# Attention scores by pairs of key blocks: full passes against high queries, half passes against low queries

## The chip, the cores and the metric

The kernel runs on one core of one Trainium2 chip. The metric is the device time of one execution in microseconds (us); lower is better.

## What is computed

The kernel is a chain of three layers. The change lies in the first, an attention without softmax over 8 batches of 3072 rows:

```python
def _attn_ref(u, v, z) -> np.ndarray:
    B, S, D = u.shape            # 8, 3072, 256
    d_qk = z.shape[-1]           # 64
    scale = 1.0 / S
    scores = scale * np.matmul(z, z.transpose(0, 2, 1))
    attn = np.maximum(scores, 0.0) ** 2
    out = np.matmul(attn, v)
    return (u * out).astype(np.float32)
...
    x = attn_out.reshape(B * S, D)
    x = _moe_ref(x=x, **moe_kwargs)
    return _moe2_ref(x=x, **moe2_kwargs)
```

Queries and keys are the same z, so the scores are symmetric. `_moe_ref` is a dense layer (256 to 1024, softmax-like gate, layer norm, back to 256), `_moe2_ref` routes each row to one of 8 experts.

## The kernel before

**Precision.** All data is float32. A float32r matmul rounds its inputs, so each operand is split into a high part (the rounded value) and a low part (the rest). A product of two split operands is three matmuls, high with high, high with low, low with high (`mm3`, L107 to L110).

**Tiling.** Queries go by chunks of 512 (`CH`), six a batch, 48 in all (`NCHUNK`). Keys go by blocks of 128 rows (`P`), 24 for each chunk (`NKB`), so the attention has 48 x 24 = 1152 slots. One slot handles one key block of one chunk. For the block of slot n the scores are computed four slots ahead (`LA`), ScalarE takes the Relu out of PSUM (`act_relu`, L432), squares it and rounds it to ah (L437, L442), VectorE makes the low part al (L447), and TensorE adds six matmuls to the chunk's output o (`pe_av`, through L108 to L110).

**Symmetry.** A block whose mirror image has been computed for an earlier chunk of the batch is not computed again: it was kept in DRAM, is fetched three slots ahead (`get`, L410) and transposed by VectorE where needed. Of a batch's 144 slots 88 are computed, 704 in all. The buffers through which kept blocks go out and come back are a ring (`sym_b`, L349 to L352) of `NSYM` = 8; each write and each fetch takes the next place of the ring (`sym`, L383).

**The scores.** z has only 64 columns. `load_z` puts the transposed chunk of z twice on the 128 partitions, and `prep_z` (L282) turns the upper 64 into the high part and the lower 64 into the low part: the tile zw is [high; low]. `swap_z` (L296) lets GpSimd write the same chunk upside down for the queries: zv is [low; high]. A score block is then two matmuls over all 128 rows (`pe_scores`, L421): zw's block against zw gives high x high + low x low, and against zv high x low + low x high. Each score block is a PSUM buffer of its own; `ps_s` has two of them (L142), so that the scores of a computed block wait for the Relu of the computed block before the last.

**Order.** Nothing is scheduled by a tool. The loop at the end (L1047) walks the slots and issues for each, in this order, the scores of slot n + 4 (if that block is computed), the steps that were entered for this slot (the dense layer of the chunk before, the loads, `prep_z`, `swap_z` five slots before a chunk's first scores), `pe_av` of slot n, then Relu, square and split. Each engine works through its instructions in that order. The routed experts come after the attention, from about 3070 us on; they reuse the buffers of zw and zv (`take`, L764).

Of the kernel before, what the change touches and what calls it, by code (L numbers as in the profile page):

```python
# [10 lines left out]
F32 = mybir.dt.float32  # L11
F32R = mybir.dt.float32r
# [4 lines left out]
AF = mybir.ActivationFunctionType  # L17
ALU = mybir.AluOpType
# [3 lines left out]
P = 128  # L22
CH = 512
# [10 lines left out]
def attention_moe_kernel(ctx, tc, u, v, z, w_in, w_out, g_ln, w_gate, w1, w2, out):  # L34
    nc = tc.nc
    B, S, D = u.shape
    DZ = z.shape[2]
# [6 lines left out]
    NCB = S // CH  # L44
    NKB = S // P
# [3 lines left out]
    NA = 4  # L49
    ZB = 5  # L50
    GA = 3
    NSYM = 8
    PD = 1
    ZL = 8
    XA, XT0, XE = 2, 21, 23
# [45 lines left out]
    V, A, G, T = nc.vector, nc.scalar, nc.gpsimd, nc.tensor  # L101
# [30 lines left out]
    with ExitStack() as st:  # L132
        wts = st.enter_context(tc.tile_pool(name="wts", bufs=1))
        zp = st.enter_context(tc.tile_pool(name="zp", bufs=NCB))
# [7 lines left out]
        ps_s = st.enter_context(tc.tile_pool(name="ps_s", bufs=2, space=PSUM))  # L142
# [21 lines left out]
        t = vp.tile([P, 2, 4, D], F32R, tag="vw", name="raw64").bitcast(I32).rearrange("p a r d -> p (a r d)")  # L164
        raw64 = [t[:, i * 2 * CH:(i + 1) * 2 * CH].rearrange("p (f two) -> p f two", two=2) for i in range(2)]
        t = mp.tile([P, F], F32, tag="pT", name="cu64").bitcast(I32)
        c64, u64 = t[:, :CH], t[:, CH:]
        t = [mp.tile([P, CH], F32R, tag=k, name="t64").bitcast(F32) for k in ("pth0", "ptl0", "pth1", "ptl1")]
# [92 lines left out]


        z_raw, v_raw, u_raw = {}, {}, {}
        z_t, z2_t, v_t = {}, {}, {}

        def rows(x, c):
            b, j = divmod(c, NCB)
# [12 lines left out]
            z_raw[c] = w  # L280

        def prep_z(c):  # L282
            zt = z_raw.pop(c)
            up_, low = slice(0, DZ), slice(DZ, 2 * DZ)
            w = zp.tile([P, CH], F32R, tag="zw", name="zw")
            A.activation(out=w, in_=zt, func=AF.Copy)
            if c == 0:
                w2_ = zp.tile([P, CH], F32R, tag="zv", name="zv", bufs=2)
                A.activation(out=w2_, in_=zt, func=AF.Copy)
                z2_t[c] = w2_  # L290
            V.tensor_tensor(out=w[low], in0=zt[low], in1=w[low].bitcast(F32), op=ALU.subtract)
            if c == 0:
                V.tensor_tensor(out=w2_[up_], in0=zt[up_], in1=w2_[up_].bitcast(F32), op=ALU.subtract)
            z_t[c] = w

        def swap_z(c):  # L296

            w = zp.tile([P, CH], F32R, tag="zv", name="zv", bufs=2)
            G.tensor_scalar(out=w[:DZ], in0=z_t[c][DZ:], scalar1=1.0, scalar2=1.0, op0=ALU.mult, op1=ALU.mult)
            G.tensor_scalar(out=w[DZ:], in0=z_t[c][:DZ], scalar1=1.0, scalar2=1.0, op0=ALU.mult, op1=ALU.mult)  # L300
            z2_t[c] = w

        def load_v(c, h):
            t = raw.tile([P, 2, D], F32, tag="vr", name="vr", bufs=2)
# [31 lines left out]
        def again(q, k):  # L336
            return q == NCB - 2 and k == NCB - 1
# [11 lines left out]
        t = [xrow.tile([P, KD * CH], F32, tag="x", name="sym") for _ in range(2)]  # L349
        t = [x[:, i * CH:(i + 1) * CH] for x in t for i in range(2)]  # L350
        t += [mp.tile([P, CH], F32, tag=f"sym{i}", name=f"sym{i}") for i in range(NSYM - 4)]
        sym_b = t  # L352
# [13 lines left out]
        def block(n):  # L366

            c, i = divmod(n, NKB)
            kb = orders[c][i]
            return (c // NCB) % 2, c % NCB, kb // 4, kb % 4  # L370

        def is_kept(n):
            _, q, k, _ = block(n)
            return k < q and not again(k, q)
# [44 lines left out]
        s_t, r_t, a_t, ah_t, al_t, o_t = {}, {}, {}, {}, {}, {}  # L419

        def pe_scores(n):  # L421
            c = n // NKB
            _, _, k, r = block(n)
            w = z_t[(c // NCB) * NCB + k][:, r * P:(r + 1) * P]
            s = ps_s.tile([P, CH], F32, tag="s", name="s")
            T.matmul(out=s, lhsT=w, rhs=z_t[c], start=True, stop=False)
            T.matmul(out=s, lhsT=w, rhs=z2_t[c], start=False, stop=True)  # L427
            s_t[n] = s

        def act_relu(n):  # L430
            r = ap.tile([P, CH], F32, tag="r", name="r")
# [323 lines left out]
        def own(pool, tag, shape, dt=F32R, bufs=None):  # L755
            return pool.tile(shape, dt, tag=tag, name=tag + "_x", **({"bufs": bufs} if bufs else {}))

        def own_vp():
            return own(vp, "vw", [P, 2, 4, D]).rearrange("p a r d -> p (a r d)")

        def cut4(t):
            return [t[:, i * CH:(i + 1) * CH] for i in range(4)]

        def take(name):  # L764

            if name in ("raw1", "raw2"):
                raw_w[name] = own_vp().bitcast(F32)
            elif name in ("w1h", "w1l", "w2h", "w2l"):
                w_set[0, name] = cut4(own_vp())
            elif name == "xT0":  # L770
                xT_t[0] = own_vp().rearrange("p (a k c) -> p a k c", a=2, k=KD)
            elif name == "xT1":
                xT_t[1] = own(mp, "xt", [P, 2, KD, CH])
            elif name == "hT":
                t = [own(zp, "zw", [P, CH]) for _ in range(NCB)]
                t += [own(zp, "zv", [P, CH], bufs=2) for _ in range(2)]
                hT_b.extend((t[i], t[i + 1]) for i in range(0, len(t) - 1, 2))
                o_b.extend(own(ap, "a", [P, CH], F32, bufs=NA).rearrange("p (r d) -> p r d", d=D) for _ in range(2))
            elif name == "out":
                t = own(mp, "p", [P, F], F32)  # L780
                o_b.extend(t[:, i * CH:(i + 1) * CH].rearrange("p (r d) -> p r d", d=D) for i in range(2))
            elif name == "set1":
                c = [own(raw, "zd", [P, CH], F32)]
                t = own(raw, "ur", [P, KD, CH], F32)
                c += [t[:, 0], t[:, 1]]
                c += [own(ap, "r", [P, CH], F32) for _ in range(2)] + [own(ap, "a", [P, CH], F32, bufs=NA), own(mp, "sym0", [P, CH], F32)]
                c += [own(mp, f"sym{i}", [P, CH], F32) for i in (1, 2)]
                c = [t.bitcast(F32R) for t in c]
                c += [own(ap, "ah", [P, CH], bufs=4) for _ in range(4)]
                c += [own(ap, "al", [P, CH], bufs=3) for _ in range(3)]  # L790
                for i, k in enumerate(("w1h", "w1l", "w2h", "w2l")):
                    w_set[1, k] = c[4 * i:4 * i + 4]
# [50 lines left out]
        for i in range(NU):  # L843
            w = HALF if i < N_CUT else units[i]
# [71 lines left out]
        for c in range(NCHUNK):  # L916
# [8 lines left out]
            else:  # L925
# [5 lines left out]
                at(base - 2, turn_z, c)  # L931
            at(zload, load_z, c)
            at(base, prep_z, c)
            if c > 0:
                at(s0 - LA - 5, swap_z, c)
# [12 lines left out]
            for t in range(4):  # L948
                w = s1 + 2 + (TW if last else 6) * t
# [8 lines left out]
                out_, back, cut_, y = (4, 6, 10, 12) if last else (5, 8, 12, 15) if c < NCHUNK - 3 else (5, 7, 10, 12)  # L958
                at(w + out_, blk_put, c, t)
                at(w + back, blk_get, c, t)  # L960
                cut_, y = w + cut_, w + y
# [32 lines left out]

        s0 = NS - NKB
        at(s0, take, "raw1")
        at(s0, load_w, 0, 1)
        at(s0 + 6, take, "w1h")
        at(s0 + 11, take, "w1l")
        at(s0 + 16, take, "raw2")  # L1000
        at(s0 + 16, load_w, 0, 2)
# [44 lines left out]
        with tc.manual_schedule():  # L1046
            for n in range(min(lo_slot, -LA), hi_slot + 1):  # L1047
                i = n + LA
                k = n - NS
                if 0 <= i < NS and not is_kept(i):  # L1050
                    pe_scores(i)
# [59 lines left out]
```

## Time and profile before

| | |
|---|---|
| median of 3 runs (lowest, highest) | 4315.48 us (4313.22, 4316.8) |
| profiled execution: own time, span of its core | 4313.29 us, 4311.6 us |
| TensorE, matmuls: busy, share, count | 4231.3 us, 98%, 23458 |
| TensorE, weight loads: busy, share | 3664.3 us, 85% |
| VectorE / ScalarE / GpSimd: share of the span | 74% / 65% / 28% |
| chain that ended last: TensorE, DMA, SP's queue, VectorE | 75%, 7%, 7%, 6% |

Rows of the profile name the line of the kernel, the engine (PE is TensorE, PEld its weight loads, DVE VectorE, ACT ScalarE, POOL GpSimd, SP the queue of the sync engine, which issues most DMAs), the operation, and output<-inputs by the program's names with their shapes. In a timeline the first number is the start and the second the length, in us. The end of a matmul is modelled: the next one can start before it. In a group, "xN | a, b | c" is N instructions, a us of busy time, b ns of one on average, and c us in which the engine stood idle just before them, with what ended that after "<-".

### The profile page before, as it was taken

The numbers are of one execution on the slowest core, as the hardware profiler recorded it, in microseconds if no ns is written. First come the engines' busy times: TensorE is split into PE (matmuls) and PEld (weight loads), VectorE is DVE, ScalarE is ACT, GpSimd is POOL, SyncE is SP. The second block draws the span as 40 slices with busy tenths as digits, with TensorE's granted clock in tenths as the row PEclk, the third lists the DMA queues.
The fourth block names the chain that finished last, engine by engine and source line by source line (L and its number), as shares of the span: only waits on it lengthen the run. The fifth ranks groups of instructions, "written<-read, shape, count | busy, mean of one in ns | idle before, by whom it ended". The sixth has DMA issues, their size and how long they took to land.

```text
span 4311.6 us, 74509 instructions
## 1 busy us (share of the span) xinstructions
PE 4231.3 (98%) x23458; PEld 3664.3 (85%) x23458; DVE 3197.2 (74%) x5624; ACT 2800.7 (65%) x5184; POOL 1200.7 (28%) x2486
## 2 busy tenths in 40 slices
PE   7999999999999999999999999999899999999999
PEld 5888888888888888888888888888788999999998
DVE  8777787777778787877877787777666656655686
ACT  6766776776677677667767766775444444444565
POOL 5023223322322332232233233323222111111111
PEclk9999999999999999999999999999999999999999
DMA  5799789889978988897898899789755655555575
GB/s 150 169 171 167 184 174 163 178 177 175 159 192 173 163 180 180 172 161 192 172 164 183 173 174 162 186 166 165 145 147 150 156 145 134 145 137 146 155 212 170
DMA packets 2465549, 719.23 MB, mean 167 GB/s; under 512 B 2261117, under 2 KB 2351485, under 8 KB 2465152
## 3 DMA queue, kind: packets, MB, share of 16 engines
q1 hardware_dynamic: 2441952, 654.93, 72.9%
q0 software_dynamic: 23200, 59.55, 4.4%
q8 instruction: 183, 3.00, 0.3%
q14 instruction: 214, 1.75, 0.1%
HBM read 442.46 MB, written 273.49 MB: 166 GB/s over the span
## 4 chain that ended last, share of the span: by engine, by line
PE 75%; DMA 7%; SPq 7%; DVE 6%; issue 2%; ACT 2%; POOL 0%; DVEq 0%; POOLq 0%; ACTq 0%
PE o L109 10%; PE o L108 10%; PE o L110 9%; SPq L410 4%; PE y L109 3%; PE y L108 3%; PE y L110 3%; PE g L108 3%; PE yp L108 3%; PE g L109 3%; PE yp L110 3%; PE yp L109 3%; PE h L494 3%; PE h L495 3%; PE h L498 3%; PE g L110 3%
## 5 line engine op out<-in xcount | busy, mean ns | idle before, releaser
L109 PE MATMUL o<-al,vw 128*128 128x512 f32 x2304 | 912.8, 396 | 26.6 <-DVE al L447 26.0
L108 PE MATMUL o<-ah,vw 128*128 128x512 f32 x2304 | 910.4, 395 | 3.0 <-DVE ut L471 2.8
L110 PE MATMUL o<-ah,vw 128*128 128x512 f32 x2304 | 900.7, 391 | 0.0
L442 ACT ACTIVATE ah<-a 128x512 fp32r<-128x512 f32 x832 | 526.0, 632 | 201.1 <-DVE a L416 77.1
L432 ACT ACTIVATE r<-s 128x512 f32<-128x512 f32 x704 | 415.3, 590 | 344.8 <-PE s L427 327.1
L447 DVE TENSOR_TENSOR al<-a,ah 128x512 fp32r<-128x512 f32 x832 | 575.5, 692 | 1.0
L109 PEld LDWEIGHTS o<-al,vw 128*128 128x128 f32 x2304 | 434.6, 189 | 122.0 <-DVE al L447 44.1
L110 PEld LDWEIGHTS o<-ah,vw 128*128 128x128 f32 x2304 | 434.9, 189 | 93.8
L108 PEld LDWEIGHTS o<-ah,vw 128*128 128x128 f32 x2304 | 434.7, 189 | 88.0 <-issue 2.7
L105 DVE TENSOR_TENSOR ptl<-pT,pth 128x512 fp32r<-128x512 f32 x384 | 264.2, 688 | 267.5 <-ACT pth L104 266.5
L108 PE MATMUL yp<-gw,pth 128*128 128x264 f32 x1536 | 440.1, 286 | 13.5 <-ACT pth L104 13.5
L437 ACT ACTIVATE a<-r 128x512 f32<-128x512 f32 x704 | 437.6, 622 | 12.9 <-DVE al L447 11.2
L110 PE MATMUL yp<-gw,ptl 128*128 128x264 f32 x1536 | 438.8, 286 | 0.9 <-DVE ptl L105 0.9
L869 ACT ACTIVATE zw_x<-g 128x512 fp32r<-128x512 f32 (+1 forms) x350 | 183.0, 523 | 393.6 <-PE g L110 390.0
L109 PE MATMUL yp<-gw,pth 128*128 128x264 f32 x1536 | 438.5, 285 | 0.0
L870 DVE SCALAR_TENSOR_TENSOR zw_x<-g,zw_x 128x512 fp32r<-128x512 f32 (+1 forms) x350 | 208.3, 595 | 266.2 <-ACT zw_x L869 260.9
L663 POOL DMA_INDIRECT sorted_rows<-y,pi x192 | 206.5, 1076 | 426.0 <-DMA sorted_rows<-y,pi 375.4
L104 ACT ACTIVATE pth<-pT 128x512 fp32r<-128x512 f32 x384 | 237.8, 619 | 123.4 <-DMA pT<-moved 123.3
L108 PEld LDWEIGHTS yp<-gw,pth 128*128 128x128 f32 x1536 | 289.7, 189 | 30.2 <-ACT pth L104 15.5
L495 PE MATMUL h<-w_in,xt 128*128 128x512 f32 x768 | 304.7, 397 | 0.0
L494 PE MATMUL h<-w_in,xt 128*128 128x512 f32 x768 | 304.4, 396 | 0.0
L109 PEld LDWEIGHTS yp<-gw,pth 128*128 128x128 f32 x1536 | 290.7, 189 | 14.4
(276 smaller groups left out, 10641.7 us busy)
## 6 DMA issues: line engine op xcount, KB each, us to landing
vw_x<-in_moe_w SPq DMA_DIRECT2D x124, 1024.0 KB
sym<-kept SPq DMA_DIRECT2D x1792, 64.0 KB
moved<-pb SPq DMA_DIRECT2D x768, 128.0 KB
pT<-moved SPq DMA_DIRECT2D x768, 128.0 KB
kept<-sym SPq DMA_DIRECT2D x320, 256.0 KB
kept<-a SPq DMA_DIRECT2D x128, 256.0 KB
vr<-in_v SPq DMA_DIRECT2D x96, 256.0 KB
x<-sorted_rows SPq DMA_DIRECT2D x328, 64.0 KB
```

Source lines behind the costliest of these rows:

```text
L104: A.activation(out=hi, in_=src, func=AF.Copy)
L105: V.tensor_tensor(out=lo, in0=src, in1=hi.bitcast(F32), op=ALU.subtract)
L108: T.matmul(out=out, lhsT=lh, rhs=rh, start=start, stop=False, **kw)
L109: T.matmul(out=out, lhsT=lh, rhs=rl, start=False, stop=False, **kw)
L110: T.matmul(out=out, lhsT=ll, rhs=rh, start=False, stop=stop, **kw)
L432: A.activation(out=r, in_=s_t.pop(n), func=AF.Relu)
L437: A.activation(out=a, in_=r_t.pop(n), func=AF.Square)
L442: A.activation(out=h, in_=a_t[n], func=AF.Copy)
L447: V.tensor_tensor(out=l, in0=a_t[n], in1=ah_t[n].bitcast(F32), op=ALU.subtract)
L494: T.matmul(out=h[:, fs], lhsT=w[:, 0, kd, ts_], rhs=w_in_t[0][:, kd, fs], start=(kd == 0), stop=False)
L495: T.matmul(out=h[:, fs], lhsT=w[:, 0, kd, ts_], rhs=w_in_t[1][:, kd, fs], start=False, stop=False)
L870: V.scalar_tensor_tensor(out=lo, in0=h, scalar=0.0, in1=hi.bitcast(F32), op0=ALU.max, op1=ALU.subtract)
```

## The change

The scores of a chunk's computed blocks are now made two at a time. Of each chunk's z the key blocks are laid out in turn: an even block of 128 columns is [high; low], an odd one [low; high]; for that `prep_z` makes two subtractions of half the columns instead of one. The queries are two tiles, zh = [high; high] and zl = [low; low], which `swap_z` copies out of zw with eight GpSimd instructions of 64 partitions x 256 columns, in place of two of 64 x 512. For a pair (an even block and the next computed block, an odd one) `pe_scores` takes both PSUM buffers and issues four matmuls: each block over all 128 rows against zh (high x high + low x high), then each block's high half alone, 64 rows, against the same 64 rows of zl (high x low). The even block's high half lies on partitions 0 to 63 and the odd one's on 64 to 127; as built, the half matmuls name a tile of 64 x 128 of the array at row 0 and at row 64. The product low x low is left out. At the slot of the pair's second block nothing is issued. The ring of buffers for kept blocks has seven places instead of eight.

```diff
...
     GA = 3
-    NSYM = 8
+    NSYM = 7
     PD = 1
...
         z_raw, v_raw, u_raw = {}, {}, {}
-        z_t, z2_t, v_t = {}, {}, {}
+        z_t, zq_t, v_t = {}, {}, {}
...
         def prep_z(c):
             zt = z_raw.pop(c)
...
             if c == 0:
-                w2_ = zp.tile([P, CH], F32R, tag="zv", name="zv", bufs=2)
-                A.activation(out=w2_, in_=zt, func=AF.Copy)
-                z2_t[c] = w2_
-            V.tensor_tensor(out=w[low], in0=zt[low], in1=w[low].bitcast(F32), op=ALU.subtract)
+                zh, zl = q_tiles(c)
+                A.activation(out=zh, in_=zt, func=AF.Copy)
+            for i, half in enumerate((low, up_)):
+                x, y = [t.rearrange("p (r two k) -> p r two k", two=2, k=P)[half, :, i] for t in (zt, w)]
+                V.tensor_tensor(out=y, in0=x, in1=y.bitcast(F32), op=ALU.subtract)
             if c == 0:
-                V.tensor_tensor(out=w2_[up_], in0=zt[up_], in1=w2_[up_].bitcast(F32), op=ALU.subtract)
+                V.tensor_tensor(out=zl, in0=zt, in1=zh.bitcast(F32), op=ALU.subtract)
             z_t[c] = w
+        def q_tiles(c):
+            zq_t[c] = [zp.tile([P, CH], F32R, tag=k, name=k, bufs=2) for k in ("zh", "zl")]
+            return zq_t[c]
         def swap_z(c):
-            w = zp.tile([P, CH], F32R, tag="zv", name="zv", bufs=2)
-            G.tensor_scalar(out=w[:DZ], in0=z_t[c][DZ:], scalar1=1.0, scalar2=1.0, op0=ALU.mult, op1=ALU.mult)
-            G.tensor_scalar(out=w[DZ:], in0=z_t[c][:DZ], scalar1=1.0, scalar2=1.0, op0=ALU.mult, op1=ALU.mult)
-            z2_t[c] = w
+            zw = z_t[c].rearrange("p (r two k) -> p r two k", two=2, k=P)
+            for low, w in enumerate(q_tiles(c)):
+                w = w.rearrange("p (r two k) -> p r two k", two=2, k=P)
+                for half in range(2):
+                    for odd in range(2):
+                        at_ = odd ^ low
+                        G.tensor_scalar(out=w[half * DZ:(half + 1) * DZ, :, odd],
+                                        in0=zw[at_ * DZ:(at_ + 1) * DZ, :, odd],
+                                        scalar1=1.0, scalar2=1.0, op0=ALU.mult, op1=ALU.mult)
...
         def pe_scores(n):
+            if n in s_t:
+                return
             c = n // NKB
-            _, _, k, r = block(n)
-            w = z_t[(c // NCB) * NCB + k][:, r * P:(r + 1) * P]
-            s = ps_s.tile([P, CH], F32, tag="s", name="s")
-            T.matmul(out=s, lhsT=w, rhs=z_t[c], start=True, stop=False)
-            T.matmul(out=s, lhsT=w, rhs=z2_t[c], start=False, stop=True)
-            s_t[n] = s
+            zh, zl = zq_t[c]
+            pair = [n, next(i for i in range(n + 1, (c + 1) * NKB) if not is_kept(i))]
+            ws = []
+            for i, x in enumerate(pair):
+                _, _, k, r = block(x)
+                assert r % 2 == i
+                ws.append(z_t[(c // NCB) * NCB + k][:, r * P:(r + 1) * P])
+                s_t[x] = ps_s.tile([P, CH], F32, tag="s", name="s")
+            for x, w in zip(pair, ws):
+                T.matmul(out=s_t[x], lhsT=w, rhs=zh, start=True, stop=False)
+            for i, (x, w) in enumerate(zip(pair, ws)):
+                half = slice(i * DZ, (i + 1) * DZ)
+                T.matmul(out=s_t[x], lhsT=w[half], rhs=zl[half], start=False, stop=True)
...
                 t = [own(zp, "zw", [P, CH]) for _ in range(NCB)]
-                t += [own(zp, "zv", [P, CH], bufs=2) for _ in range(2)]
+                t += [own(zp, "zh", [P, CH], bufs=2) for _ in range(2)]
                 hT_b.extend((t[i], t[i + 1]) for i in range(0, len(t) - 1, 2))
```

On TensorE, in the first chunk of the fifth batch (about 1550 us of the profile before), each block's two passes stood ahead of the six matmuls of o of their slot (s are scores, ah, al and vw the split operands of the output; a chunk's o is two tiles):

```order
L426 MATMUL s<-zw 128x512
L427 MATMUL s<-zv,zw 128x512
...
L108 MATMUL o_18681<-ah,vw 128x512
L109 MATMUL o_18681<-al,vw 128x512
L110 MATMUL o_18681<-ah,vw 128x512
L108 MATMUL o_18685<-ah,vw 128x512
L109 MATMUL o_18685<-al,vw 128x512
L110 MATMUL o_18685<-ah,vw 128x512
L426 MATMUL s<-zw 128x512
L427 MATMUL s<-zv,zw 128x512
```

In the changed program, at the same place, the four passes of a pair stand in one slot, and behind that slot's matmuls of o come other steps (yp, of the dense layer) at once ("x2" is two in a row):

```order
L448 MATMUL s<-zh,zw 128x512 x2
L451 MATMUL s<-zl,zw 128x512 x2
...
L108 MATMUL o_18880<-ah,vw 128x512
L109 MATMUL o_18880<-al,vw 128x512
L110 MATMUL o_18880<-ah,vw 128x512
L108 MATMUL o_18884<-ah,vw 128x512
L109 MATMUL o_18884<-al,vw 128x512
L110 MATMUL o_18884<-ah,vw 128x512
L108 MATMUL yp<-gw_139,pth_18934 128x264
```

Two passes of a later slot have moved ahead of one slot's six matmuls of o, and the half passes stand behind both full ones. On GpSimd the copies for the next chunk stand in the midst of the steps that scale a chunk's rows (vv and tt); before:

```order
L583 TENSOR_TENSOR vv<-vv,q 128x4
L584 TENSOR_SCALAR vv<-vv 128x4
L299 TENSOR_SCALAR zv<-zw 64x512
L300 TENSOR_SCALAR zv<-zw 64x512
L597 TENSOR_TENSOR tt<-rs 128x4
```

And in the changed program at the same place:

```order
L606 TENSOR_TENSOR vv<-vv,q 128x4
L607 TENSOR_SCALAR vv<-vv 128x4
L311 TENSOR_SCALAR zh<-zw 64x2x128 x4
L311 TENSOR_SCALAR zl<-zw 64x2x128 x4
L620 TENSOR_TENSOR tt<-rs 128x4
```

The place in the queue is the same; four instructions into zh and four into zl stand there for two into zv.

## Rows read from the trace of the kernel before

**Rows 1.** The page: busy time of TensorE; its busy tenths in 40 slices.

```profile
PE 4231.3 (98%) x23458; PEld 3664.3 (85%) x23458; DVE 3197.2 (74%) x5624; ACT 2800.7 (65%) x5184; POOL 1200.7 (28%) x2486
...
PE   7999999999999999999999999999899999999999
```

**Rows 2.** Stages (start:end, length in us; busy us and count by engine; clock; DMA).

```profile
core 0: us, PE busy (x) PEld busy (x) DVE busy (x) ACT busy (x) POOL busy (x), PEclk, DMA share, GB/s
...
800.00:1600.00 800.00, 797.17 (x4048) 674.36 (x4047) 628.73 (x1068) 577.44 (x1037) 254.43 (x598) 1.00 0.86 176
...
3070.00:4311.60 1241.60, 1215.91 (x8300) 1126.62 (x8298) 803.08 (x1535) 628.66 (x1283) 252.22 (x299) 0.99 0.59 154
```

**Rows 3.** Groups by line (count, busy us, mean ns, idle before): scores on TensorE.

```profile
L426 PE MATMUL s<-zw 128*128 128x512 f32 x704 | 278.1, 395 | 16.0 <-ACT r L432 8.7 <-DVE zw L291 7.3
...
L427 PE MATMUL s<-zv,zw 128*128 128x512 f32 x704 | 276.8, 393 | 0.0
```

**Rows 4.** Timeline (start, length us, engine) of one block's scores in a steady stretch.

```profile
1504.74 0.39 PE L426 MATMUL s<-zw 128*128 128x512 f32 x1
...
1504.74 0.19 PEld L427 LDWEIGHTS s<-zv,zw 128*128 128x128 f32 x1
...
1504.97 0.39 PE L427 MATMUL s<-zv,zw 128*128 128x512 f32 x1
...
1505.19 0.40 PE L494 MATMUL h<-w_in,xt 128*128 128x512 f32 x1
```

**Rows 5.** Timeline of TensorE and its weight loads (PEld) behind a wait.

```profile
1500.70 0.19 PEld L109 LDWEIGHTS o<-al,vw 128*128 128x128 f32 x1 [1.03 <-DVE al L447]
...
1500.71 0.50 PE L109 MATMUL o<-al,vw 128*128 128x512 f32 x1 [0.61 <-DVE al L447]
...
1500.81 0.19 PEld L110 LDWEIGHTS o<-ah,vw 128*128 128x128 f32 x1
...
1501.04 0.39 PE L110 MATMUL o<-ah,vw 128*128 128x512 f32 x1
...
1501.04 0.19 PEld L108 LDWEIGHTS o<-ah,vw 128*128 128x128 f32 x1
```

**Rows 6.** Timeline of TensorE where bf16 matmuls of 32 columns stand between others.

```profile
230.25 0.39 PE L110 MATMUL o<-ah,vw 128*128 128x512 f32 x1
230.49 0.19 PE L648 MATMUL rk<-oh,upper 128*128 128x32 bf16 x1
230.52 0.18 PE L649 MATMUL rk<-cum,ones 128*128 128x32 bf16 x1
230.55 0.47 PE L108 MATMUL o<-ah,vw 128*128 128x512 f32 x1
```

**Rows 7.** Timeline of ScalarE's Relu and TensorE's scores, at the start and end.

```profile
14.65 0.79 PE L426 MATMUL s<-zw 128*128 128x512 f32 x1 [4.99 <-ACT r L432]
...
15.53 0.59 ACT L432 ACTIVATE r<-s 128x512 f32<-128x512 f32 x1
...
3061.68 0.59 ACT L432 ACTIVATE r<-s 128x512 f32<-128x512 f32 x1
...
3062.03 0.39 PE L426 MATMUL s<-zw 128*128 128x512 f32 x1
```

**Rows 8.** Preparing z: timeline at chunk 1, then lines of similar instructions.

```profile
77.40 0.69 POOL L300 TENSOR_SCALAR zv<-zw 64x512 fp32r<-64x512 f32 x1
...
86.41 0.39 PE L426 MATMUL s<-zw 128*128 128x512 f32 x1
...
L609 POOL TENSOR_SCALAR y<-y,rs x192: 479/486/1447, 206.2 to 3238.0; 128x256 f32<-128x256 f32 x192
...
L870 DVE SCALAR_TENSOR_TENSOR zw_x<-g,zw_x 128x256 fp32r<-128x256 f32 x122 | 50.7, 416 | 25.6 <-ACT zw_x L869 25.2
...
L291 DVE TENSOR_TENSOR zw<-zt,zw 64x512 fp32r<-64x512 f32 x48 | 34.2, 714 | 7.8 <-ACT zw L286 6.4
```

**Rows 9.** SP's event waits at the fetch of kept blocks (ns: least, median, most).

```profile
L410 SPq EVENT_SEMAPHORE  x38: 17/17/2292, 210.0 to 3048.5; - x38
```


## Prediction, made before the changed kernel was run

> **What bounds the kernel now.** I read the page first. TensorE is busy nearly all of the span, and the busy tenths are 9 in almost every slice [rows 1]. The table of stages then tells the two parts of the program apart. From 130 us to about 3070 us the attention loop runs. TensorE is busy for 797.17 of 800 us in the middle stretch at a granted clock of 1.00, the 2.4 GHz level; VectorE has 628.73, ScalarE 577.44, the DMA engines a share of 0.86 [rows 2]. A busy share of TensorE does not say that every matmul is needed, so I went to the timeline for the pace: a full 128x512 matmul starts 0.23 us after the one before it, and its weight load starts together with the matmul before it, so that it costs nothing [rows 4]. The row shows a matmul as 0.39 us long, but the next starts after 0.23 us: the last 0.16 us are a tail that normally lies under the next matmul. In steady stretches these starts follow each other without a hole, so the attention part is bound by TensorE's stream of matmuls, and a matmul less is 0.227 us less, as long as nothing else comes late.
>
> The scores are two of these matmuls for each computed key block: 704 and 704 [rows 3], 1408 x 0.227 = 320 us in all. This is the whole stock that the change works on.
>
> **The passes that go.** Before, a pair of computed blocks is four full passes. After, it is two full passes and two half passes. The matmul count is unchanged, 352 pairs of four. If the two half passes run at the same time, a pair is three passes long and 352 x 0.227 = 79.9 us leave TensorE's path. If they run one after the other, nothing leaves. No matmul of the program before uses less than 128 rows, so the trace shows neither, and I bound it by the nearest rows.
>
> *The second half's weights.* Where TensorE had waited, the next two weight loads start at 1500.70 and 1500.81, and the third only at 1501.04, when the second matmul starts [rows 5]. Weights are loaded one matmul ahead, and a load that nothing hides takes 0.11 us. There the matmul of 1500.71 is 0.50 us instead of 0.39 and the next one follows after 0.33 instead of 0.23 us. If the load of the second half can only begin when the first half starts, the second half starts 0.11 us behind it, and a pair saves 0.227 - 0.11 = 0.117 us: 352 x 0.117 = 41.2 us. If it goes ahead, because it fills the other 64 rows, the pair saves the whole 0.227 us. I take the load as exposed, since every load in the trace goes exactly one ahead, and keep both ends.
>
> *The change from full to half and back.* There are 704 such changes, two a pair. At the low end a change costs nothing: where a bf16 matmul of other size follows a float32r one, it starts at the usual 0.24 us, and the next but 0.03 us later [rows 6]; a gain below that I exclude, as a change has nothing to leave out. One end above is the load that cannot go ahead, 0.11 us each [rows 5]. The other is that the array must first run empty: 0.39 - 0.227 = 0.16 us of tail each [rows 4], and both together 0.27. I take nothing, by the row that is a change of kind in mid-stream, and keep the others as rivals, since that row changes type and width but not the rows of the array. The Trainium skill speaks against me here (TensorEngine Tiling (Array Packing), Tiling Modes, Key Properties): changing the tiling mode, not only the tile, drains TensorE. No row of this case shows such a change; by that rule the sum comes out as in the second rival. The same skill (TensorE: Matmul & The Clock Gate, Part 3, The mechanism) has matmuls on different row groups start some 4 ns apart; no row here shows that either, and by it the sum would be the first rival's.
>
> **Two buffers asked for at once.** The scores have two buffers. Before, block n waits for the Relu (act_relu, L432) of two computed blocks back; TensorE or its weight load hardly ever wait for it. After, a pair needs both, so it waits for the Relu of the block just before. I set the start of every second L426 beside the end of the Relu before it. In 31 of 351 places that Relu ends later than the pair would start, by 30.8 us in sum: 19.1 us of it in 11 places before 115 us, 11.7 us in 20 places at the turns from one batch to the next and at the end. The first and the last are in [rows 7]: 15.53 + 0.59 against 14.65, and 3061.68 + 0.59 against 3062.03. Queued behind such a wait on TensorE are the six matmuls of o of the slot, and for those VectorE and ScalarE wait by the buffers of ah and al. Ends: 0, as in all these places the Relu starts right behind other work of ScalarE, and TensorE would have waited for ScalarE's next result anyway; and 31 us. At the start of the program ScalarE sets the pace, so I count nothing there and half of the 11.7 us later: 6 us. On the other side the second Relu of a pair finds its scores ready; that is idle time of ScalarE, which is not the bound, and I count nothing. The first Relu finds them one pass later (0.23 us), which the four blocks of lookahead hide; without them it would be 352 x 0.23 = 81 us.
>
> **The preparation of z.** GpSimd wrote one swapped tile with two instructions, of 0.69 us in [rows 8]; now it writes two tiles with eight instructions of half the columns. Half of 0.69 is 0.35 us, and a 256-column instruction of GpSimd takes 0.49 us in the median, so eight are between 8 x 0.35 = 2.8 us and 8 x 0.49 = 3.9 us, against 1.4 us: 1.4 to 2.5 us more per chunk [rows 8]. GpSimd is no bound; its queue behind it holds the small steps of scaling and routing, for which nobody in the loop waits. The tightest place is chunk 1: the second instruction ends at 78.09, and the chunk's first score starts at 86.41 [rows 8], so 8.3 us cover 2.5. Without that cover it would be 47 x 2.5 = 118 us. VectorE has two subtractions of half the columns for one of 0.714 us. At 0.416 us each [rows 8] that is 0.12 us more, 6 us over 48 chunks, on an engine with a fifth of its time free. Chunk 0 makes its low tile with one more subtraction, under 0.8 us, while TensorE still waits for input. Price of these: 0; end of the range +1.
>
> **One buffer less for kept blocks.** The ring has seven instead of eight. A block is fetched three slots ahead and read until two slots after its copy; one ring place is used per block at most, so seven places are still a longer stretch than a buffer's life. SP's event waits at the fetch are 38, of 17 ns in the median [rows 9]. Price 0. If the cover fails, a fetch is late by a slot now and then; the queue then also holds the writes of kept and moved blocks. TensorE would wait behind ah and al. I have no count for that and put it under the range's upper part.
>
> **The sum.** -41.2 + 6 = -35 us. The profiled execution took 4313.29 us (span 4311.6), 2.2 us under the median of the runs, 4315.48. On the median: 4280 us. The measurement of this kernel can tell about 0.2%, 9 us, from no change.
>
> **The rivals.** *All of the pass goes.* The second half's weights are loaded ahead of the first half. -79.9 + 6 = -74: 4242 us, and 4236 without the waits. For it: in [rows 5] two loads follow each other at 0.11 us, and two of them fit under one full pass of 0.227. Against: the third load waits for the matmul. *The array runs empty at each change: slower.* Place: the 704 borders between full and half passes, on TensorE itself. Price: 0.16 us each, 0.32 a pair, against 0.227 saved if the halves lie side by side: +0.093 x 352 + 6 = +39, 4354 us; with the second load exposed too it is (0.32 - 0.117) x 352 + 6 = +77, 4393 us. It decides from 0.11 us per change (0.06 with the exposed load). For it: half the array is used in another shape, and the sums of the pass before are still under way for 0.16 us. Against: types and widths change in the trace without a hole. This is where the Trainium skill's draining rule leads (TensorEngine Tiling (Array Packing), Key Properties). *Weights cannot be loaded across a change:* 0.22 us a pair against 0.227: -2 + 6 = +4, 4319 us. *It does not do what it says:* the halves run one after the other, nothing else changes: +6, 4321 us, both within 0.2%.
>
> **How the numbers follow.** Forecast (second half 0.11 us behind, free change): 0.35. All of the pass: 0.22. Run empty: 0.31, of it 0.17 near 4354 and 0.14 near 4393 and above. Weights not loaded across: 0.07. One after the other: 0.05. So faster 0.57, within 0.2% 0.12, slower 0.31. Likeliest case's own range, by the waits of 0 to 31 us: 4274 to 4305. The range over the cases goes from 4236 (all of the pass, no wait) to 4370, over 4354 with some of the waits; it leaves out the dearer kind of run-out, 0.14, and little below.
>
> **What the changed kernel's profile would show.** Forecast: of the two half passes (L451) the second starts 0.11 us after the first, the next full matmul about 0.23 us after that, and the first half 0.23 us after the full pass. All of the pass: the starts of the halves nearly coincide. Run empty: the first half starts 0.39 us after the last full pass, and the next full matmul 0.39 us after a half. One after the other: 0.23 us apart. For the waits: idle time of TensorE before the first pass (L448) for the Relu of about 6 us past the start-up; many times more would prove that term wrong. GpSimd's copies must end before the chunk's first score. What makes the prediction wrong is a pace at the changes other than 0.23 us, above all.

## The result: slower by 1.4%

The changed kernel takes 4374.74 us in the median (4372.53 to 4382.55, 4 runs) beside 4315.79 us of the kernel before; the ratio is 1.014, with a 95% interval of 1.0124 to 1.0156. The forecast was 4280 us, faster, with a range up to 4370. The result is on the second rival's side, between its two prices of 4354 and 4393 us and 5 us above the range. The profiled execution has a span of 4372.7 us.

The page and the stages of the changed kernel, where [rows 1, 2] showed those of before (start:end, length; busy us and count by engine; clock; DMA):

```profile
PE 4290.5 (98%) x23458; PEld 3573.8 (82%) x23458; DVE 3195.9 (73%) x5672; ACT 2795.6 (64%) x5184; POOL 1322.3 (30%) x2768
...
800.00:1600.00 800.00, 796.82 (x3971) 636.62 (x3970) 620.56 (x1071) 567.43 (x1021) 274.95 (x645) 1.00 0.85 172
```

TensorE is as busy as before and its clock is granted at the 2.4 GHz level, as before. But in the same 800 us it gets through 3971 matmuls in place of 4048, although a pair of half passes should have made room for more. The busy share hides the loss. The groups of the scores (count, busy us, mean ns, idle before and what ended it) show where to look:

```profile
L448 PE MATMUL s<-zh,zw 128*128 128x512 f32 x704 | 224.3, 396 | 30.3 <-ACT r L455 23.5 <-ACT zh L290 6.6
L451 PE MATMUL s<-zl,zw 64*128 64x512 f32 x704 | 178.2, 503 | 0.0
...
L451 PEld LDWEIGHTS s<-zl,zw 64*128 64x128 f32 x704 | 66.1, 184 | 123.5 <-issue 120.9 <-POOL tt L622 1.8 <-DVE zl L295 0.5
```

The half passes are recorded 503 ns long, against 393 of a full one in [rows 3], and their weight loads stand idle for 123.5 us first, 120.9 of them waiting for nothing that the profile shows ("issue"). One pair in the timeline (start, length; "x2" is two in a row, shown as one stretch), first TensorE's weight loads, then its matmuls:

```profile
1002.58 0.19 PEld L451 LDWEIGHTS s<-zl,zw 64*128 64x128 f32 x2 [0.35 <-issue]
1003.01 0.19 PEld L108 LDWEIGHTS o<-ah,vw 128*128 128x128 f32 x1 [0.24 <-issue]
1003.12 0.19 PEld L109 LDWEIGHTS o<-al,vw 128*128 128x128 f32 x1
```

```profile
1002.04 0.61 PE L448 MATMUL s<-zh,zw 128*128 128x512 f32 x2
1002.59 0.50 PE L451 MATMUL s<-zl,zw 64*128 64x512 f32 x2
1003.01 0.50 PE L108 MATMUL o<-ah,vw 128*128 128x512 f32 x1
1003.35 0.40 PE L109 MATMUL o<-al,vw 128*128 128x512 f32 x1
```

Read them against [rows 4, 5]. Two half passes take one stretch of 0.50 us, as long as one of them: they do run side by side, and their weights are loaded side by side too. In all 352 pairs the second is recorded 3 to 4 ns after the first. But the first half's weights are not loaded under the last full pass. That pass began at about 1002.26 (the stretch of two is 0.61 us long, a single one 0.39), and the load begins at 1002.58, 0.32 us later in the median of all pairs, where it used to be at the same moment. Since nothing hides the load, its 0.11 us come on top: the pass is 0.50 us long instead of 0.39, as behind a wait in [rows 5]. On the way out the same happens again. The next load of a full pass begins 0.43 us after the halves were recorded, 0.32 after they really start, and its 0.11 us are exposed again: the next matmul follows after 0.34 us instead of 0.23.

So each change of the array's shape costs 0.32 - 0.23 = 0.09 us until the next weights begin to load, and 0.11 us because they are not loaded ahead: 0.20 us. I read the 0.09 us as the run-out, the time until the pass before has left the array; the trace shows the start of the load, not the array itself. A pair has two changes and saves one pass, 2 x 0.20 - 0.227 = +0.17 us, and 352 x 0.17 = +60 us. The measured medians differ by 59 us. That the two agree so closely is in part luck: by the runs below the rest of the change adds about 14 us, and the changes of shape come through in the time with about as much less than the starts say.

### The profile page after: what moved, and what is told of

Same layout as the page of the kernel before. It is cut to its first block, busy times and chain, and to the rows that moved or that the text cites. A ratio compares the mean times of both kernels' runs of the same rounds, so it can differ in the third digit from the quotient of the medians.

```text
span 4372.7 us, 75087 instructions
## 1 busy us (share of the span) xinstructions
PE 4290.5 (98%) x23458; PEld 3573.8 (82%) x23458; DVE 3195.9 (73%) x5672; ACT 2795.6 (64%) x5184; POOL 1322.3 (30%) x2768
## 4 chain that ended last, share of the span: by engine, by line
PE 77%; DMA 8%; SPq 6%; DVE 5%; issue 2%; ACT 1%; POOL 1%; DVEq 0%; POOLq 0%; ACTq 0%
PE o L108 10%; PE o L109 10%; PE o L110 9%; PE h L517 4%; PE yp L108 4%; PE yp L109 3%; PE y L108 3%; PE yp L110 3%; PE y L110 3%; PE y L109 3%; PE g L108 3%; PE h L521 3%; PE h L518 3%; PE g L109 3%; PE g L110 3%; PE s L448 3%
## 5 line engine op out<-in xcount | busy, mean ns | idle before, releaser
L108 PEld LDWEIGHTS o<-ah,vw 128*128 128x128 f32 x2304 | 434.4, 189 | 98.9 <-issue 17.8
L108 PE MATMUL yp<-gw,pth 128*128 128x264 f32 x1536 | 451.4, 294 | 12.7 <-ACT pth L104 12.7
L109 PE MATMUL yp<-gw,pth 128*128 128x264 f32 x1536 | 438.9, 286 | 0.0
L465 ACT ACTIVATE ah<-sym 128x512 fp32r<-128x512 f32 x320 | 201.7, 630 | 231.3 <-PE o L110 109.4
L533 DVE TENSOR_REDUCE nm<-h 128x1 f32<-128x1024 f32 x192 | 234.6, 1222 | 146.2 <-PE h L521 137.5
L108 PEld LDWEIGHTS yp<-gw,pth 128*128 128x128 f32 x1536 | 290.6, 189 | 51.3 <-issue 26.3
L517 PE MATMUL h<-w_in,xt 128*128 128x512 f32 x768 | 321.2, 418 | 0.0
```

The lines of the kernel that those rows point to most:

```text
L108: T.matmul(out=out, lhsT=lh, rhs=rh, start=start, stop=False, **kw)
L109: T.matmul(out=out, lhsT=lh, rhs=rl, start=False, stop=False, **kw)
L465: A.activation(out=h, in_=a_t[n], func=AF.Copy)
L517: T.matmul(out=h[:, fs], lhsT=w[:, 0, kd, ts_], rhs=w_in_t[0][:, kd, fs], start=(kd == 0), stop=False)
L533: V.tensor_reduce(out=s["nm"][:, t:t + 1], in_=h, axis=AX.X, op=ALU.max, negate=True)
```

## Experiments

The theory (A in the texts below): the change of shape costs 0.20 us, whatever stands on its sides. Rivals: the rest of the change costs it (B); a half pass as such costs it (C); a pass over a part of the rows costs it (D). The runs came in three groups. Each group has its own runs of the kernel before beside it on the same chip (medians 4315.41, 4321.19 and 4324.04 us), so I compare ratios to the kernel before and turn them into us with 4315.5 us.

**Full low passes.** The pairs stay and everything around them; only the shape goes.

```diff
-                half = slice(i * DZ, (i + 1) * DZ)
-                T.matmul(out=s_t[x], lhsT=w[half], rhs=zl[half], start=False, stop=True)
+                T.matmul(out=s_t[x], lhsT=w, rhs=zl, start=False, stop=True)
```

> The changed kernel with one thing undone: the second pass of each block of a pair is again a full pass over all 128 rows against zl (high x low + low x low); pairs, their order, the two buffers asked for at once, the copies of z and the ring of seven stay. Theory A (each change between full and half passes costs 0.20 us, 0.09 until the array has run out and 0.11 for weights that are not loaded ahead; the halves lie side by side): no change of shape is left, so 4316 us and a few us of waits, 4313 to 4322. Rival B (the loss comes from the rest: pairs need both score buffers, GpSimd copies more, the ring is shorter): about 4375 us, as slow as the changed kernel. Rival C (each half pass as such costs 0.20 us more than a full one, wherever it stands): 4316 us as A.

Measured: 4330.16 us, 1.0032 (1.0021 to 1.0044). More than A's few us, far from B's 4375: three quarters of the loss go with the half passes, and 14 us are left that belong to the rest. What they are is taken up below.

**Every second pair.**

```diff
+            n_pair[0] += 1
...
-                half = slice(i * DZ, (i + 1) * DZ)
+                half = slice(i * DZ, (i + 1) * DZ) if n_pair[0] % 2 else slice(0, P)
```

> The changed kernel in which only every second pair has half passes (176 of 352); the other pairs have full low passes. Theory A: 176 x (2 x 0.20 - 0.227) = +30 us over the kernel before, 4346 us, half of the way. Rival B: about 4375 us, as nothing else is changed. Rival C: 4346 us as A.

Measured: 4353.99 us, 1.0089 (1.0072 to 1.0105). It lies in the middle between the run with no half passes (1.0032) and the changed kernel (1.014). The loss grows with the number of visits to the other shape.

**Four changes a pair.** The same matmuls, in another order.

```diff
-            for x, w in zip(pair, ws):
-                T.matmul(out=s_t[x], lhsT=w, rhs=zh, start=True, stop=False)
             for i, (x, w) in enumerate(zip(pair, ws)):
                 half = slice(i * DZ, (i + 1) * DZ)
+                T.matmul(out=s_t[x], lhsT=w, rhs=zh, start=True, stop=False)
                 T.matmul(out=s_t[x], lhsT=w[half], rhs=zl[half], start=False, stop=True)
```

> The changed kernel with the order inside a pair changed to full, half, full, half: four changes of shape a pair instead of two, and no two half passes next to each other. Work and result are the same. Theory A: nothing is saved and 4 x 0.20 = 0.80 us a pair added, 352 x 0.80 = +282 us, 4598 us. Rival C (a price of each half pass, not of the change): two half passes of 0.227 + 0.20, +0.40 us a pair, 4457 us. Rival B: about 4375 us.

Measured: 4561.63 us, 1.0569 (1.0548 to 1.059), +246 us over the kernel before and +232 over the run with full low passes. C's 4457 is out by 105 us, A's 4598 by 36. The timeline of one pair, matmuls of TensorE:

```profile
1004.13 0.39 PE L449 MATMUL s<-zh,zw 128*128 128x512 f32 x1
1004.45 0.50 PE L450 MATMUL s<-zl,zw 64*128 64x512 f32 x1
1004.87 0.49 PE L449 MATMUL s<-zh,zw 128*128 128x512 f32 x1
1005.30 0.49 PE L450 MATMUL s<-zl,zw 64*128 64x512 f32 x1
1005.72 0.39 PE L108 MATMUL yp<-gw,pth 128*128 128x264 f32 x1
1005.95 0.28 PE L109 MATMUL yp<-gw,pth 128*128 128x264 f32 x1
```

Every step between a full and a half pass is 0.42 to 0.43 us (0.32 where the load before it was hidden), in both directions alike, and each pass on the far side is longer by its load, even the 264-column one (0.39 instead of 0.28). By these starts a pair takes 1004.13 to 1005.72 = 1.59 us, and 0.11 more for the load behind it, against 4 x 0.227 = 0.91: +0.79 us, 278 us in all. In the time 46 of them are missing; they are taken up below.

**Both halves on the same rows.** For the odd block this multiplies low by low in place of high by low.

```diff
-                half = slice(i * DZ, (i + 1) * DZ)
+                half = slice(0, DZ)
```

> The changed kernel with both half passes on the upper 64 rows of the array, where they cannot run at the same time; for the odd block this multiplies low by low in place of high by low, so its result is less exact. Two changes of shape a pair remain. Theory A: the saving of 0.227 us a pair goes and the changes stay, 4316 + 352 x 0.40 = 4457 us. If the halves of the changed kernel only look simultaneous in the trace and run one after the other: 4375 us, no difference.

Measured: 4441.03 us, 1.029 (1.0269 to 1.031); +65 us against the changed kernel, where A expected 80 and "not simultaneous" none. So the halves of the changed kernel did run side by side. The timeline:

```profile
1003.12 0.73 PE L451 MATMUL s<-zl,zw 64*128 64x512 f32 x2
1003.77 0.39 PE L108 MATMUL yp<-gw,pth 128*128 128x264 f32 x1
```

Two halves on the same rows are a stretch of 0.73 us, 0.23 more than the 0.50 of two on different rows. That is the usual pace, so the weights of the second are loaded under the first: inside a shape, loading ahead works as ever.

**Four halves in one visit.** The half passes are issued twice, so that the product high x low is added twice.

```diff
-            for i, (x, w) in enumerate(zip(pair, ws)):
-                half = slice(i * DZ, (i + 1) * DZ)
-                T.matmul(out=s_t[x], lhsT=w[half], rhs=zl[half], start=False, stop=True)
+            for j in range(2):
+                for i, (x, w) in enumerate(zip(pair, ws)):
+                    half = slice(i * DZ, (i + 1) * DZ)
+                    T.matmul(out=s_t[x], lhsT=w[half], rhs=zl[half], start=False, stop=j == 1)
```

> The changed kernel with the two half passes of a pair issued twice in a row, so four half passes between the same two changes of shape; the high x low product is added twice, so the scores are slightly off. Theory A (the price hangs on the change, not on the half pass): one more round of 0.227 us for two halves side by side, 352 x 0.227 = +80 us over the changed kernel, 4455 us; inside the visit the halves follow each other at 0.227 us without a hole. Rival C (a price of about 0.18 us on each half pass): 352 x (0.227 + 2 x 0.18) = +207 us, 4581 us.

Measured: 4436.76 us, 1.027 (1.0248 to 1.0291); against the changed kernel's 1.014 that is +56 us. A said 80, C 207. The timeline shows the four in the same 0.73 us stretch that two on the same rows took:

```profile
1002.54 0.73 PE L452 MATMUL s<-zl,zw 64*128 64x512 f32 x4
1003.20 0.39 PE L108 MATMUL yp<-gw,pth 128*128 128x264 f32 x1
```

A second round in the same visit costs no more than a pass (0.73 - 0.50 = 0.23 us). The price belongs to the change.

**96 rows.** The even block's low pass uses 96 rows; half of its low x low product is left out.

```diff
-                half = slice(i * DZ, (i + 1) * DZ)
+                half = slice(0, P if i else 96)
```

> As the run with full low passes (4330 us), but the low pass of the even block uses 96 of the 128 rows; such a matmul still takes the whole array as its tile, so no change of shape occurs. The even blocks' low x low product is cut to half of its rows. Theory A (the change of the array's tile costs, not that rows lie idle): 4330 us, the same as with full low passes, and the starts stay 0.227 us apart. Rival D (a pass over a part of the rows makes the next weights wait): one such border in and one out in each pair at 0.16 to 0.20 us, +113 to +141 us, 4443 to 4471 us.

Measured: 4340.36 us, 1.0047 (1.0031 to 1.0063); the interval overlaps that of full low passes (1.0021 to 1.0044) and the time is far from D's 4443. Idle rows alone do not cost it:

```profile
1001.75 0.62 PE L448 MATMUL s<-zh,zw 128*128 128x512 f32 x2
1002.20 0.63 PE L451 MATMUL s<-zl,zw 96*128 96x512 f32 x2
1002.67 0.28 PE L108 MATMUL yp<-gw,pth 128*128 128x264 f32 x1
```

Two full passes, two low passes and the next matmul start 0.45 and 0.47 us apart, 0.23 each, and the matmul behind is 0.28 us long: its load was hidden. A small cost is left: over all pairs the steps behind the two low passes are 0.233 and 0.238 us in the median instead of 0.227, 0.017 us a pair and 6 us in all, as much as the time is longer than with full low passes (1.0047 against 1.0032).

**What the rest costs.** Three runs split the 14 us of the run with full low passes. The first keeps zh, zl and the ring of seven but issues each block in its own slot:

```diff
-            pair = [n, next(i for i in range(n + 1, (c + 1) * NKB) if not is_kept(i))]
...
+            T.matmul(out=s_t[n], lhsT=w, rhs=zh, start=True, stop=False)
+            T.matmul(out=s_t[n], lhsT=w, rhs=zl, start=False, stop=True)
```

> As the run with full low passes (4330 us), but each block's two passes are issued in its own slot again, as in the kernel before; the copies into zh and zl by eight GpSimd instructions and the ring of seven stay. It tells what made the run with full low passes 15 us slower than the kernel before. If it is that a pair asks for both score buffers at once (TensorE's idle time for the Relu grew from 10 to 33 us in the trace): back to 4315 us, 4312 to 4319. If it is the copies of z or the shorter ring: 4330 us, no change.

Measured: 4329.24 us, 1.0017 (1.0008 to 1.0027). On this chip the kernel before takes 4321.19 us; at 4315.5 the ratio is 4323 us, between the two expectations. (The text above has the wait for the Relu grow from 10 to 33 us; the rows of the matmuls have 8.7 us before, [rows 3], and 28.0 with full low passes.) Then the kernel before with one part each, `NSYM = 7` alone, and the pairing alone:

> The kernel before with the ring of buffers for kept blocks cut from eight to seven, nothing else. The run with single blocks, zh and zl, and seven buffers was 1.0017 of the kernel before (1.0008 to 1.0027). If the ring makes that, this run shows 1.0017, 4322 to 4323 us. If the GpSimd copies make it: 1.000, 4315 us.

> The kernel before with only the pairing: at the slot of a pair's first block both blocks' passes against zw, then both against zv, all four over 128 rows; zw, zv, the two GpSimd copies and the ring of eight stay. If asking for both score buffers at once costs what the prediction put on it, 6 us: 4321 us, 1.0014. If all of the loss of the run with full low passes (1.0032) comes from pairing: 4329 us. If nothing of it: 4315 us.

Measured: the ring of seven 4322.08 us, 0.9994 (0.9985 to 1.0003), no difference. The pairing alone 4333.54 us, 1.0022 (1.0013 to 1.0031), +9.5 us (6 to 13). In the trace of that run TensorE's scores wait 28.1 us for the Relu, where [rows 3] had 8.7; the run with a ring of seven, on the same chip and without pairs, has 10.1. First the pairing alone, then the ring of seven:

```profile
L432 PE MATMUL s<-zw 128*128 128x512 f32 x704 | 225.0, 397 | 35.4 <-ACT r L438 28.1 <-DVE zw L291 7.2
L109 PE MATMUL o<-al,vw 128*128 128x512 f32 x2304 | 912.9, 396 | 18.1 <-DVE al L453 17.8
```

```profile
L426 PE MATMUL s<-zw 128*128 128x512 f32 x704 | 277.8, 395 | 17.0 <-ACT r L432 10.1 <-DVE zw L291 6.9
L109 PE MATMUL o<-al,vw 128*128 128x512 f32 x2304 | 912.3, 396 | 30.8 <-DVE al L447 30.4
```

The 18 us more of waiting for the Relu are not all lost, for the wait of o for al falls by 12.6. Up to 130 us the two cancel (Relu 9.3 to 19.1 us, al 12.6 to 4.0), and TensorE has started the same 397 matmuls by then in both runs. Behind 130 us the Relu's wait grows from 0.8 to 8.9 us and al's falls only from 17.8 to 13.8. So the loss arises later; these two rows show 4.1 us of it net, and the rest is not placed.

Some 7 us remain with the new layout of z (GpSimd's eight copies, VectorE's two subtractions, the one more tile of queries), since the ring is cleared. Which of these it is, and through what wait, the runs do not show. One trace each cannot place it either: the run with single blocks has a span 8.5 us longer than the ring of seven, and 5.9 of them lie behind the last score; but that stretch also differs by 6.7 us (1249.0 and 1255.7) between the run with four halves and the one with every second pair, which have the same instructions there. The preparation itself is not late: in the changed kernel the copies took 0.428 and 0.543 us each, 3.9 us a chunk, as the upper bound had it, and over all chunks they ended at least 6.7 us before the chunk's first score.

```profile
L311 POOL TENSOR_SCALAR zl<-zw 64x256 fp32r<-64x256 f32 x188 | 102.0, 543 | 13.3
L311 POOL TENSOR_SCALAR zh<-zw 64x256 fp32r<-64x256 f32 x188 | 80.4, 428 | 32.9 <-DMA sorted_rows<-y,pi 25.9
```

**Where the starts say more than the time.** Taken from whole times beside the run with full low passes, a change costs (1.0569 - 1.0032) x 4315.5 / 1408 = 0.165 us with four changes a pair, 0.158 with both halves on the same rows (704 changes and no saving), and in the changed kernel (47 + 80) / 704 = 0.18; in the starts it is 0.20. A likely reason is that where TensorE is held up longer the others come less late. Its idle time before the second matmul of o, for al, in the run with full low passes, in the changed kernel and with four changes a pair:

```profile
L109 PE MATMUL o<-al,vw 128*128 128x512 f32 x2304 | 912.0, 396 | 18.5 <-DVE al L469 18.4
```

```profile
L109 PE MATMUL o<-al,vw 128*128 128x512 f32 x2304 | 909.6, 395 | 12.9 <-DVE al L470 12.8
```

```profile
L109 PE MATMUL o<-al,vw 128*128 128x512 f32 x2304 | 908.1, 394 | 6.2 <-DVE al L469 6.0
```

The wait of the scores for the Relu fell likewise, from 28.0 us to 23.5 and 14.3. With four changes the two make 12 + 14 = 26 of the 46 us; where the rest went is not shown.

No version beat the kernel before. As an estimate from the measured prices, a visit to the half shape (0.40 us) pays from two rounds on: four blocks at once would save 2 x 0.227 - 0.40 = 0.05 us, 176 x 0.05 = 10 us, before the waits and the 7 us of the layout. That needs four score buffers at a time where the kernel has two; it wasn't tried.

## Why the prediction was wrong, point by point

- **What bounds the kernel:** right. TensorE's stream sets the time; a pass more or less within a shape moved it by most of 0.227 us a pair (65 us of 80 with the halves on the same rows, 56 with four halves).
- **The second half's weights:** wrong, on the dear side. They were forecast 0.11 us behind; the halves start 3 to 4 ns apart, as in the first rival. The rule of loading one matmul ahead came from loads that all fill the same 128 rows. The Trainium skill (TensorE: Matmul & The Clock Gate, Part 3, The mechanism) had 4 ns, and the trace agrees.
- **The change from full to half and back:** this is the step that failed. I took nothing, by a row in which type and width change [rows 6], and said myself that it does not change the rows of the array. The nearest row in looks was not near in kind. The bounds above were 0.11 (load exposed), 0.16 (run empty) and 0.27 (both); measured is both, with 0.11 for the load as priced and 0.09 for the run-out, where the recorded tail of 0.16 overstated it: 0.20. The mechanism is that of two rivals at once, the array that runs empty (4354 us) and the weights that are not loaded across a change (4319 us). Their sum was named as a bound, 0.27 us, but got no time and no chance; it would have been (2 x 0.27 - 0.227) x 352 + 6 = +116 us, 4432. The 4393 us added something else, the second half's load, which did not occur; that the result lies between 4354 and 4393 is therefore no success of that rival. The range ended 5 us below the result. The Trainium skill (TensorEngine Tiling (Array Packing), Tiling Modes, Key Properties) has the rule that a change of tiling mode drains TensorE; the 0.09 us before each load agree with it.
- **Two buffers at once:** 6 us forecast, 9.5 measured (6 to 13), by the wait that was named and in the stretch that was named: nothing net up to 130 us, 8.1 us more wait for the Relu behind it, where the forecast had found 11.7 and counted half. Of the 9.5 us the rows show 4.1 net behind 130 us, so it is right in kind, too small by a third, and not wholly placed. In the changed kernel itself the Relu's wait behind 130 us is 4.8 us, where about 6 was named as the sign.
- **The preparation of z:** 0 forecast, at most 1; some 7 us measured. The cover of the first score held (6.7 us at the least), so the cost is elsewhere and open.
- **One buffer less:** 0 forecast, none measured.
- **What would show it:** the list had the right place. It named a pace at the changes other than 0.23 us as what would prove the forecast wrong; it was 0.32 with a load of 0.11 behind it.

## What to carry to other kernels

Price a change in the shape of the array like an instruction of its own, here 0.20 us in and 0.20 us out, and count visits, not passes: at these shapes, halves side by side pay only when one visit saves more than 0.40 us. When an operation is not in the trace, a row that merely changes something is no evidence for it; ask whether it changes the same thing, and add the bounds where two causes can hold at once. In a timeline of TensorE read the starts and the weight loads, since the busy share was 98% before and after.

## What the runs showed of the hardware that was not expected

- Two float32r matmuls of 64 x 128 tiles on the two halves of the array run at once, weights included: 3 to 4 ns between their starts over 352 pairs, and a stretch of 0.50 us for two, where two on the same rows take 0.73.
- A change between a 128-row and a 64-row tile costs the same in both directions, 0.09 us before the weights begin to load and 0.11 us of exposed load, while 96-row matmuls among 128-row ones cost 0.02 us a pair (0.233 and 0.238 us from start to start).
- A cost on the engine that sets the pace did not come through in full: 0.20 us a change in the starts became 0.16 to 0.18 us in the time.
